# Moving two output products and four base products inside the last head group of an attention kernel

## The chip, the cores and the metric

One core of a Trainium2 chip runs the program. The metric is the device time of one execution in microseconds (us). Five engines work side by side, each through its own instruction queue in order: PE (TensorE: matmuls, and weight loads that run ahead of them), ACT (ScalarE), DVE (VectorE), POOL (GpSimd) and SP, which here only issues DMAs. They wait for one another with semaphores.

## The reference

```
xn = layernorm(A_x)                                   # 2048 x 512
q  = (xn @ wq) as 32 heads of 128
p  = softmax(q k^T / sqrt(128)) ; o = p v             # per head, 2048 keys
s  = concat(o) @ wo                                   # 2048 x 4096 @ 4096 x 512
gate = xn @ W_gate ; up = xn @ W_up
g  = silu((relu(gate) * up) @ W_down)
out = A_x + s * g
```

## The kernel before

The work runs in 128 *blocks*, one for each pair of a head and a quarter of the queries (512 of them). A block has 8 *positions*. At a position PE computes a pair of score tiles (`emit_S_tile`, L1626: two 512-column matmuls) for the position three ahead, ACT turns such a pair into `PT` with one exponential (L1638), and PE multiplies the `PT` of its own position with V (`emit_PV_tile`, L1735: eight matmuls). At the end of a block DVE divides by the row sums (`emit_norm_block`: reciprocal L1655, multiply L1658), and SP transposes the result into `OT_store` by DMA (L1663). The first PV matmul of the next block waits for that multiply, because it overwrites the same accumulator.

All other matrix work is put between these positions as *items* by a plan that is written out by hand: `at(block, position, item)` and `put_p0` fill `plan`, and `side` holds work for DVE, POOL and SP. The loop goes through the blocks position by position and emits, in this order: the score pair, the items of the position, the side work, the PV matmuls. Every engine executes its own instructions in the order of emission.

The accumulators of score pairs and items are three slots of PSUM, taken in turn (`ring_acquire`). Whoever takes a slot waits on PE until the work that last read it is done: the exponential for a score pair, the additions on DVE for an item. When the item at position 0 of a block is marked early (all `emit_x`, `emit_xd` and one-bank items are), the next score pair is emitted right behind it.

Sixteen blocks are four heads, a *head group*. While one group's attention runs, the output product of the group before it is computed by a seven-product scheme of 2 x 2 blocks. The last group, blocks 112 to 127, carries that of group 6; "r3" below is block 112 + 3. Plain products (`emit_one`, L1458, products 1, 7 and 4) take two matmuls of 512 columns for each bank, and DVE adds each bank to two sums at once (`acc`, L1389). Products with a second level (`emit_x`, L1523) take five matmuls, and their remainder (`emit_xd`, L1554 and L1555) two more. The sums are the four tiles `s_acc[:, J, i]`, J from 0 to 3.

Sums that are complete become *base* products: `emit_base(J, i)` multiplies one quarter of a sum by g on DVE (`scalar_tensor_tensor`, L1587), and POOL adds x to it (L1592). g and x had been moved out to DRAM and come back transposed, as `gT` and `xT`. The function `reload_g` issues these DMAs on SP: its first half stands at r3 position 5, its second half at r5 position 1. Each half is four transposing DMAs, gT and xT in turn (L1146, L1147). The wait of a base product reads

```
_wait_all(dve, [os_tok[(J, i)], sem_gr.cur()])
```

where `sem_gr.cur()` stands for every gT reload that was issued before this point of the program, not for the columns that the product reads. The products (0, 0) to (0, 3) read the column groups 0 and 1 of gT, which are those of the first half.

SP's queue in these blocks holds, in order: the K load for the head that starts at r8 (L366; it is emitted at r3 position 5 and waits for the last score pair of the head before, which PE computes at r3 position 4), the first half of the reload, a V load (L371), the transposes of r3 and r4 (L1663), the second half, a load of gN (L1149), and the transposes of r5 and r6.

Of the kernel before, what the change touches and what calls it, by code (L numbers as in the profile page):

```python
# [52 lines left out]
def bass_recurrent_scan__mha_block_cached__glu_gated_reglu__prompt_kernel(  # L53
# [63 lines left out]
    with ExitStack() as es:  # L117
# [1361 lines left out]
        left = {}  # L1479
# [381 lines left out]
        def at(b, p, *items):  # L1861
            plan.setdefault((b, p), []).append(list(items))
# [5 lines left out]
        side = {}  # L1868
# [4 lines left out]
        def put_p0(b, it):  # L1873
            assert b not in osteps
            osteps[b] = it
            if it[0] is emit_x or it[0] is emit_xd or it[1] == 1:
                early.add(b)

        xsteps = (0, 2, 3)
        for g in range(NG - 1):  # L1880
            b0 = (g + 1) * GB
            half = g < NG - 2
            if half and g:
                order = ((2, 0), (1, 2), (7, 4), (6, 6), (5, 10), (3, 14))
                left[g] = len(order) + 4
                for k, r in ((0, 8), (2, 12), (3, 13)):
                    put_p0(b0 + r, (emit_one, 1, g, 4, k // 2, k % 2))
                at(b0 + 3, 6, (emit_one, 1, g, 4, 0, 1))
                early.add(b0 + 9)
                for j, r in order:  # L1890
                    x_at.add(b0 + r)
                    put_p0(b0 + r, (emit_x, 0, g, j, 0))
                    for k in (1, 2):
                        at(b0 + r, 5 if k == 2 and r in (2, 4) else xsteps[k], (emit_x, 0, g, j, k))
                    put_p0(b0 + r + 1, (emit_xd, 2, g, j))
                    side.setdefault((b0 + r - 2, 6 if r in (4, 6) else 4), []).append((prep_x, g, j, 0))
                    side.setdefault((b0 + r - 1, 1), []).append((prep_x, g, j, 1))
                for (r, p), c, i in (((-5, 4), 0, 0), ((-5, 4), 1, 0), ((2, 0), 0, 1), ((2, 2), 0, 2), ((3, 1), 1, 1),
                                     ((3, 3), 1, 2), ((8, 1), 0, 3), ((10, 5), 1, 3)):
                    side.setdefault((b0 + r, p), []).append((emit_ox, g, c, i))  # L1900
                moves = [((1, 2), store_sum, 0), ((4, 1), store_sum, 4), ((5, 2), load_sum, 2), ((6, 1), store_sum, 5),
                         ((6, 6), load_sum, 0)]
                if g == 1:
                    moves.append(((0, 1), store_sum, 2))
                else:
                    moves += [((0, 5), load_sum, 4), ((2, 1), load_sum, 5)]
                if g < NG - 3:
                    moves.append(((16, 1), store_sum, 2))
                for (r, p), fn, a in moves:
                    side.setdefault((b0 + r, p), []).append((fn, a))  # L1910
                continue
            split = {} if g == 0 else {3: 6} if half else {3: 5, 8: 4}
            if g == 0:
                full, part, xs = {0: (1, 0), 12: (1, 1), 2: (7, 0), 6: (7, 1)}, (1, 3, 7, 13), {2: 4, 6: 8, 5: 10, 3: 14}
            elif half:
                full, part, xs = {0: (1, 0), 2: (1, 1), 3: (7, 0), 8: (7, 1)}, (1, 9, 12, 13), {2: 4, 6: 6, 5: 10, 3: 14}
            else:
                full, part, xs = {0: (1, 0), 2: (1, 1), 3: (7, 0), 6: (7, 1)}, (1, 7), {2: 4, 6: 8, 5: 10, 3: 12}
                at(b0 + 9, 4, (emit_one, 2, g, 4, 1, 0))
            for r, (j, q) in full.items():  # L1920
                if r in split:
                    put_p0(b0 + r, (emit_one, 1, g, j, q, 0))
                    at(b0 + r, split[r], (emit_one, 1, g, j, q, 1))
                else:
                    put_p0(b0 + r, (emit_one, 2, g, j, q, 0))
            for k, r in enumerate(part):
                put_p0(b0 + r, (emit_one, 1, g, 4, k // 2, k % 2))
            left[g] = len(full) + len(split) + len(part) + 4 + (not half)
            for j, r in xs.items():
                x_at.add(b0 + r)  # L1930
                put_p0(b0 + r, (emit_x, 0, g, j, 0))
                for k in (1, 2):
                    at(b0 + r, xsteps[k], (emit_x, 0, g, j, k))
                put_p0(b0 + r + 1, (emit_xd, 2, g, j))
            px = ((2, 1), (4, 4), (7, 1), (11, 1))
            if g == 0:
                px = ((2, 1), (5, 3), (8, 5), (11, 3))
            elif not half:
                px = (px[0], ((5, 4))) + ((8, 5), (10, 5))
            for k, (j, (r, p)) in enumerate(zip((2, 6, 5, 3), px)):  # L1940
                side.setdefault((b0 + r, p), []).append((prep_x, g, j, 0))
                r, p = max((r, p), (xs[(2, 6, 5)[k - 1]] + 1, 1)) if k else (r, p)
                side.setdefault((b0 + r, p), []).append((prep_x, g, j, 1))
            ox = ((0, 0), (0, 3), (1, 0), (1, 2), (1, 3), (1, 4), (9, 6), (9, 4))
            if not half:
                ox = ((0, 2), (4, 4), (4, 5), (0, 5), (5, 2), (5, 3), (9, 2), (9, 3))
            elif g:
                ox = ((0, 2), (0, 3), (0, 4), (3, 2), (3, 3), (3, 4), (8, 5), (8, 1))
            for k, (r, p) in enumerate(ox):
                side.setdefault((b0 + r, p), []).append((emit_ox, g, *((k // 3, k % 3) if k < 6 else (k - 6, 3))))  # L1950
# [20 lines left out]
        for b in range(NBLK):  # L1971
            pr, r = (b - 2) // 8 + 1, (b - 2) % 8
# [49 lines left out]
        fb = GB * (NG - 1)  # L2022
# [3 lines left out]
                           (4, 6, 5, 2)):  # L2026
            side.setdefault((fb + r, p), []).append((add_kept, a, i))
        for i in range(4):
            side.setdefault((fb + 7, 2 + i), []).append((emit_base, 0, i))
        for i, part, (r, p) in ((1, 0, (11, 1)), (1, 1, (11, 2)), (3, 0, (11, 2)), (3, 1, (11, 3)), (0, 0, (11, 2)), (0, 1, (11, 4)), (2, 0, (11, 4)), (2, 1, (11, 5))):  # L2030
            side.setdefault((fb + r, p), []).append((emit_finish, i, part))
        for k, (J, i) in enumerate(((3, 1), (3, 3), (1, 1), (1, 3))):
# [28 lines left out]
        for gp in range(LAG, TOTP):  # L2061
# [7 lines left out]
            split = not ahead and not items and bq < GB  # L2069
# [107 lines left out]
```

## Time and profile before

| | |
|---|---|
| time, median of 3 runs | 1234.03 us (1233.92 to 1234.49) |
| the profiled execution's own time | 1233.89 us |
| its span, first to last instruction | 1232.6 us (1.29 us lie around it) |
| PE busy | 1227.8 us (100%) |
| ACT busy | 1041.9 us (85%) |
| DVE busy | 873.5 us (71%) |
| POOL busy | 834.5 us (68%) |
| granted TensorE clock | 0.999 |

The blocks are found in the trace by the reciprocal of L1655, which ends each of them: r3 ends at 1121.71 us of the span, r5 at 1137.45, r6 at 1145.39, r7 at 1153.06. Times below are us from the start of the span. Where a row merges several instructions, its time is the stretch they cover together. [...]

### The profile page before, as it was taken

The numbers are of one execution on the slowest core, as the hardware profiler recorded it, in microseconds if no ns is written. First come the engines' busy times: TensorE is split into PE (matmuls) and PEld (weight loads), VectorE is DVE, ScalarE is ACT, GpSimd is POOL, SyncE is SP. The second block draws the span as 40 slices with busy tenths as digits, with TensorE's granted clock in tenths as the row PEclk, the third lists the DMA queues.
The fourth block names the chain that finished last, engine by engine and source line by source line (L and its number), as shares of the span: only waits on it lengthen the run. The fifth ranks groups of instructions, "written<-read, shape, count | busy, mean of one in ns | idle before, by whom it ended". The sixth has DMA issues, their size and how long they took to land.

```text
span 1232.6 us, 29291 instructions
## 1 busy us (share of the span) xinstructions
PE 1227.8 (100%) x11927; PEld 817.3 (66%) x11927; DVE 873.5 (71%) x1324; ACT 1041.9 (85%) x1110; POOL 834.5 (68%) x946
## 2 busy tenths in 40 slices
PE   9999999999999999999999999999999999999998
PEld 5466666776666666666666666666666666666665
DVE  7668787667676776677666776677676767675587
ACT  4457877668899999999999999999999999989994
POOL 3355876313668767787688776986788767668368
PEclk9999999999999999999999999999999999999999
DMA  9812331323232555246522753255532562348616
GB/s 276 159 31 37 75 79 28 52 48 91 57 53 52 142 120 131 49 90 173 173 41 50 212 153 94 51 142 163 155 52 52 184 190 48 53 103 167 122 35 142
DMA packets 285061, 127.21 MB, mean 103 GB/s; under 512 B 253696, under 2 KB 279552, under 8 KB 280064
## 3 DMA queue, kind: packets, MB, share of 16 engines
q1 hardware_dynamic: 283584, 124.55, 43.6%
q8 instruction: 95, 1.56, 0.6%
q10 hardware_dynamic: 1344, 0.79, 0.2%
q14 instruction: 38, 0.31, 0.1%
HBM read 57.93 MB, written 25.17 MB: 67 GB/s over the span
## 4 chain that ended last, share of the span: by engine, by line
PE 99%; DVE 0%; DMA 0%; issue 0%
PE ps_acc L1735 38%; PE ps_r L1626 36%; PE ps_r L1060 5%; PE ps_r L1178 3%; PE ps_r L1523 3%; PE ps_r L1239 3%; PE ps_r L924 2%; PE ps_r L739 2%; PE ps_r L743 2%; PE ps_r L1458 2%; PE ps_acc L842 1%; PE ps_r L1767 1%; PE ps_r L1554 1%; PE ps_r L1555 1%; PE ps_r L1848 0%; PE ps_r L551 0%
## 5 line engine op out<-in xcount | busy, mean ns | idle before, releaser
L1638 ACT ACTIVATE PT<-ps_r 128x1024 bf16<-128x1024 f32 x1024 | 990.1, 1025 | 124.9 <-PE ps_r L1626 111.1
L1735 PEld LDWEIGHTS ps_acc<-V_sb,PT 128*128 128x128 bf16 x8192 | 544.8, 98 | 225.5 <-issue 28.1
L1735 PE MATMUL ps_acc<-V_sb,PT 128*128 128x129 bf16 x8192 | 630.0, 220 | 0.0
L1626 PE MATMUL ps_r<-QT_sb,KT_sb 128*128 128x512 bf16 x2048 | 617.6, 379 | 0.0
L1065 DVE TENSOR_TENSOR UVR<-UVR,ps_r 128x512 f32<-128x512 f32 (+1 forms) x228 | 168.8, 756 | 96.8 <-PE ps_r L1060 91.9
L1626 PEld LDWEIGHTS ps_r<-QT_sb,KT_sb 128*128 128x128 bf16 x2048 | 158.9, 98 | 35.4 <-ACT PT L1638 31.6
L1389 DVE TENSOR_TENSOR s_acc<-s_acc,ps_r 128x1024 f32<-128x1024 f32 x108 | 131.2, 1218 | 17.1 <-PE ps_r L1458 9.1
L1405 DVE TENSOR_TENSOR s_acc<-s_acc,ps_r 128x512 f32<-128x512 f32 x152 | 101.0, 683 | 28.3 <-PE ps_r L1523 23.9
L1658 DVE TENSOR_TENSOR Onorm<-ps_acc,rz_sb 128x512 bf16<-128x512 f32 x127 | 87.8, 691 | 4.4
L1489 POOL TENSOR_TENSOR TI<-OX 128x512 f16<-128x512 f16 x38 | 43.1, 1155 | 70.6 <-issue 69.2
L1655 DVE RECIPROCAL rz_sb<-ps_acc 128x4 f32<-128x4 f32 x127 | 23.1, 182 | 85.7 <-PE ps_acc L1735 84.0
L1025 POOL TENSOR_TENSOR TI<-xn_sb 128x512 f16<-128x512 f16 x48 | 55.8, 1163 | 40.7 <-PE ps_r L1060 40.7
L1065 DVE TENSOR_TENSOR QT_sb<-UVR,ps_r 128x512 bf16<-128x512 f32 x72 | 49.5, 687 | 43.0 <-PE ps_r L1060 40.6
L1489 POOL TENSOR_TENSOR TI<-OT_store 128x512 f16<-128x512 bf16 (+1 forms) x38 | 45.6, 1221 | 31.9 <-PE ps_r L1523 16.1
L1333 POOL TENSOR_TENSOR WX<-Wo_sb 128x512 f16<-128x512 bf16 x7 | 8.1, 1154 | 81.3 <-DVE Wo_sb L1323 42.4
L1025 POOL TENSOR_TENSOR TI<-xn_sb,TI 128x512 f16<-128x512 f16 x48 | 55.9, 1165 | 0.0
L1025 POOL TENSOR_TENSOR TI<-xnT 128x512 f16<-128x512 bf16 x36 | 41.6, 1155 | 14.0 <-PE ps_r L1060 14.0
L1060 PE MATMUL ps_r<-TI,SI 128*128 128x512 f16 x126 | 47.8, 379 | 0.0
L1523 PE MATMUL ps_r<-TI,SI 128*128 128x512 f16 x114 | 43.2, 379 | 0.0
L1025 POOL TENSOR_TENSOR TI<-xnT,TI 128x512 f16<-128x512 bf16 x36 | 41.6, 1155 | 0.0
L1154 POOL TENSOR_SCALAR gB<-gB 128x512 bf16<-128x512 bf16 x14 | 20.8, 1484 | 30.4 <-DVE gB L1184 30.4
L1133 POOL TENSOR_TENSOR UVR<-UVR,UVR 128x512 f32<-128x512 f32 x24 | 29.8, 1273 | 11.8 <-DVE UVR L1065 11.8
(236 smaller groups left out, 1434.6 us busy)
## 6 DMA issues: line engine op xcount, KB each, us to landing
sums<-s_acc SPq DMA_DIRECT2D x20, 1024.0 KB, 4.5
s_acc<-sums SPq DMA_DIRECT2D x18, 1024.0 KB, 5.8
V_sb<-in_A_v_cache_dram SPq DMA_DIRECT2D x32, 512.0 KB, 4.3
Wq_sb<-in_A_wq_dram SPq DMA_DIRECT2D x16, 256.0 KB, 4.5
Wo_sb<-in_A_wo_dram SPq DMA_DIRECT2D x8, 512.0 KB, 3.9
out_dram<-g_sb SPq DMA_DIRECT2D x4, 512.0 KB, 4.5
KR<-sums SPq DMA_DIRECT2D x4, 512.0 KB, 4.5
OT_store<-Onorm SPq DMA_TRANSPOSE x127, 3.0
```

The source lines that it names most:

```text
L1025: return sem_ui.sig(pool.tensor_tensor(dst, x, y, o))
L1060: return sem_up.sig(pe.matmul(dst, lhs, rhs, start=start, stop=stop, skip_group_check=True))
L1065: dve.tensor_tensor(dst, x, ps, ALU.add))
L1178: ins = pe.matmul(ps_r[:, bank, :], L(i), R(i), start=(i == 0), stop=(i == HC - 1))
L1389: t = sem_opa.sig(dve.tensor_tensor(dst, dst, sb, op))
L1405: t = dve.tensor_tensor(dst, dst, sb, op)
L1489: return sem_oi.sig(pool.tensor_tensor(dst, x, y, o))
L1523: return sem_op.sig(pe.matmul(dst, lhs, rhs, start=start, stop=stop, skip_group_check=True))
L1626: ins = pe.matmul(ps_r[:, 2 * s + tt, :], KT_sb[h % 2][:, t * 128:(t + 1) * 128], QT_sb[qt_slot[(h, Q)]][:], start=True, stop=True)
L1638: act.activation(PT[pb][:], ps_r[:, 2 * s:2 * s + 2, :], ACTF.Exp, scale=scale / WSC)
L1658: dve.tensor_tensor(Onorm[ob][:], o_ap, rz_sb[:].to_broadcast([128, 4, Dh]), ALU.mult))
L1735: ins = pe.matmul(o_ap, PT[pb][:, tt, j * 128:(j + 1) * 128], V_sb[vb][:, t, 0:VW], start=(t == 0 and j % 2 == 0), stop=(t == KT - 1 and j ...
```

## The change

Three things move, all in the last head group, and nothing is added or left out.

- Product 7 of the first query half stood with one bank at r3 position 0 and one at r3 position 5; both banks now stand at r3 position 0.
- Product 7 of the second half had both banks at r6 position 0; now one is at r6 position 0 and one at r6 position 6. Product 4 of the second half had both banks at r9 position 4; now one is at r7 position 6 and one at r9 position 6.
- The base products (0, 0) to (0, 3) stood at r7, positions 2 to 5. Now (0, 0) and (0, 1) stand at r6, positions 3 and 4, and (0, 2) and (0, 3) at r7, positions 2 and 3.

```diff
                 full, part, xs = {0: (1, 0), 2: (1, 1), 3: (7, 0), 6: (7, 1)}, (1, 7), {2: 4, 6: 8, 5: 10, 3: 12}
-                at(b0 + 9, 4, (emit_one, 2, g, 4, 1, 0))
+                split = {6: 6}
+                for r, e in ((7, 0), (9, 1)):
+                    at(b0 + r, 6, (emit_one, 1, g, 4, 1, e))
...
-            left[g] = len(full) + len(split) + len(part) + 4 + (not half)
+            left[g] = len(full) + len(split) + len(part) + 4 + 2 * (not half)
...
         for i in range(4):
-            side.setdefault((fb + 7, 2 + i), []).append((emit_base, 0, i))
+            side.setdefault((fb + 6 + i // 2, (3, 4, 2, 3)[i]), []).append((emit_base, 0, i))
```

`split` names the products whose second bank stands apart, with its position; it was `{3: 5, 8: 4}` for this group. `left[g]` only counts the products of a group, and nothing waits for the count of this one.

## The prediction

> **What bounds the kernel now.** I read the busy shares first, then the chain of waits, then the busy time of each engine block by block.
>
> ```profile
> PE 1227.8 (100%) x11927; PEld 817.3 (66%) x11927; DVE 873.5 (71%) x1324; ACT 1041.9 (85%) x1110; POOL 834.5 (68%) x946
> ...
> PE 99%; DVE 0%; DMA 0%; issue 0%
> ```
> ```profile
> 1113.76:1121.71 7.95, 7.95 (x85) 5.51 (x84) 3.27 (x5) 7.52 (x9) 6.30 (x6) 1.00 0.66 180
> ...
> 1137.45:1145.39 7.94, 7.94 (x85) 5.57 (x84) 3.18 (x5) 7.40 (x9) 2.33 (x5) 1.00 1.05 219
> 1145.39:1153.06 7.67, 7.67 (x83) 5.30 (x82) 5.46 (x7) 7.47 (x9) 4.04 (x4) 1.00 1.14 211
> ...
> 1161.35:1169.79 8.44, 8.44 (x87) 5.70 (x86) 5.84 (x7) 7.57 (x9) 2.71 (x5) 1.00 0.08 17
> ```
>
> PE never rests, and the chain is PE to 99%, so whatever makes PE wait lengthens the kernel one for one. The second fence is the table by stretch for the four blocks that the change touches, r3, r6, r7 and r9 (columns: length, then busy time of PE, weight loads, DVE, ACT, POOL, then clock, DMA share, GB/s). In r6 DVE is busy for only 3.18 of 7.94 us, which looks like room for two more instructions. That is throughput; the question is what these instructions wait for.
>
> The timelines of r6 and r7 follow, of PE, of DVE, and of SP from r3 on.
>
> ```profile
> 1137.68 1.03 PE L1458 MATMUL ps_r<-OX,WX 128*128 128x512 f16 x4
> 1138.54 0.62 PE L1735 MATMUL ps_acc<-V_sb,PT 128*128 128x129 bf16 x8
> ...
> 1145.62 0.59 PE L1458 MATMUL ps_r<-OT_store,WX 128*128 128x512 bf16 x2
> 1146.20 0.60 PE L1626 MATMUL ps_r<-QT_sb,KT_sb 128*128 128x512 bf16 x2
> ```
> ```profile
> 1146.20 0.11 PEld L1626 LDWEIGHTS ps_r<-QT_sb,KT_sb 128*128 128x128 bf16 x2 [0.48 <-ACT PT L1638]
> ...
> 1146.64 1.07 PE L1735 MATMUL ps_acc<-V_sb,PT 128*128 128x129 bf16 x16
> ```
> ```profile
> 1138.31 2.35 DVE L1389 TENSOR_TENSOR s_acc<-s_acc,ps_r 128x1024 f32<-128x1024 f32 x2
> 1145.39 0.18 DVE L1655 RECIPROCAL rz_sb<-ps_acc 128x4 f32<-128x4 f32 x1 [4.73 <-PE ps_acc L1735]
> 1145.61 0.69 DVE L1658 TENSOR_TENSOR Onorm<-ps_acc,rz_sb 128x512 bf16<-128x512 f32 x1
> 1146.25 1.22 DVE L1389 TENSOR_TENSOR s_acc<-s_acc,ps_r 128x1024 f32<-128x1024 f32 x1
> 1147.43 3.46 DVE L1587 SCALAR_TENSOR_TENSOR s_acc<-s_acc,gT 128x512 f32<-128x512 f32 x4
> ```
> ```profile
> 1118.16 2.99 SPq L366 DMA_TRANSPOSE KT_sb<-in_A_k_cache_dram  x1
> 1121.25 3.25 SPq L1146 DMA_TRANSPOSE gT<-out_dram  x1
> 1124.54 2.08 SPq L1147 DMA_TRANSPOSE xT<-in_A_x_dram  x1
> 1126.66 2.35 SPq L1146 DMA_TRANSPOSE gT<-out_dram  x1
> 1129.06 1.78 SPq L1147 DMA_TRANSPOSE xT<-in_A_x_dram  x1
> 1130.90 0.57 SPq L371 DMA_DIRECT2D V_sb<-in_A_v_cache_dram  x1
> 1131.52 4.98 SPq L1663 DMA_TRANSPOSE OT_store<-Onorm  x2
> 1136.61 2.19 SPq L1146 DMA_TRANSPOSE gT<-out_dram  x1
> 1139.14 2.22 SPq L1147 DMA_TRANSPOSE xT<-in_A_x_dram  x1
> 1141.42 2.21 SPq L1146 DMA_TRANSPOSE gT<-out_dram  x1
> 1143.67 3.10 SPq L1147 DMA_TRANSPOSE xT<-in_A_x_dram  x1
> ```
> ```profile
> gT<-out_dram SPq DMA_TRANSPOSE x1, 5.9
> xT<-in_A_x_dram SPq DMA_TRANSPOSE x1, 5.3
> ```
> ```profile
> 1149.02 5.11 POOL L1592 TENSOR_TENSOR s_acc<-s_acc,xT 128x512 f32<-128x512 f32 x4 [9.16 <-DMA xT<-in_A_x_dram]
> ```
>
> The reader is to see three things. First, SP issues without a pause from 1118.16 on; each transposing DMA holds it for about 2.2 us, and the fourth gT reload is issued only at 1141.42. The two rows on landing are those of the last gT and the last xT: they land 5.9 and 5.3 us after issue, at 1147.32 and 1148.97. POOL's row confirms the second: it waits 9.16 us for xT and starts at 1149.02, 0.05 us after the landing. Second, in the kernel before the base products start at 1147.43, 0.11 us after the last gT has landed, so their wait is paid nowhere. Third, DVE reaches the end of its additions in r6 at 1138.31 + 2.35 = 1140.66 and then sits idle, with nothing queued but the reciprocal of the block's end.
>
> **The change part by part.**
>
> *The matmuls.* Items in these four blocks take (2+2), 4, 2 and 4 plain matmuls before, and 4, (2+2), (2+2) and 2 after: 14 each time. Four cost 0.86 us (1137.68 to 1138.54), two 0.43. Sum: 0. DVE's additions move along, one of 1.22 us for each bank: also 0.
>
> *The balance with ACT.* Without items PE needs less for a position than ACT does for its exponential, so after a long plain stretch PE waits a little for a slot. At r7 the weight load shows 0.48 us of such a wait, but PE itself loses 1146.20 - (1145.62 + 0.43) = 0.15 us.
>
> ```profile
> PEld ps_r L1626 <- ACT PT L1638: 2.7, 7, 0.5
> ```
>
> That row of the waits (stretch from r3 to r10) has all seven of them, 2.7 us as the weight loads see it. Items at position 6 take this from r7 and r8. But r3 loses its item at position 5, and r6 becomes an early block; I expect about 0.15 us each at the start of r4 and of r6. If every wait is scaled as at r7 (0.15 for 0.48), all seven hold 0.8 us: bounds -0.8 and +0.3. Value: 0 up to r7, and behind it -0.2, because ACT will have caught up during the stall below.
>
> *SP's queue.* Both banks of product 7 at r3 position 0 put 0.43 us more ahead of the last score pair of the head, for which the K load waits.
>
> ```profile
> SPq L366 <- PE ps_r L1626: 3.4, 1, 3.4
> ```
>
> SP waited 3.4 us for exactly that before 1118.16 and is without a gap afterwards, so every DMA behind it goes 0.43 us later: the last gT lands at 1147.75. Bounds: 0, if the backlog swallows it, and 0.43. I take 0.43.
>
> *The base products at r6.* Here the change adds a wait. Both halves of the reload are emitted before r6, so `sem_gr.cur()` at r6 position 3 means all four gT loads. DVE comes to that instruction at about 1140 and waits until 1147.75. Queued behind it on DVE, in order: the second base product, the addition of the new item of r6 position 6, reciprocal and multiply of r6, the addition of r7's first item. PE waits for two of these: the item at r7 position 0 takes the slot that the position 6 item used (slots go in turn: item, pair of position 7, pair of r7 position 0, item), and the first PV of r7 waits for the multiply. Step by step, with 0.05 us from landing to start as on POOL:
>
> - first base product starts 1147.80; the four rows of L1587 below start between 1147.4 and 1149.2, 0.6 us apart, so the addition starts 1.2 later, at 1149.00, and takes 1.22: 1150.22;
> - reciprocal and multiply: 0.22 (1145.39 to 1145.61) plus 0.69: 1151.13;
> - from the end of a multiply to the PV matmul that waits for it: 0.19 us, as at r4 (1121.92 + 0.69 to 1122.80);
> - by the slot, PE resumes at 1150.22 + 0.19 = 1150.41, then 0.43 for the item and 0.43 for the score pair: 1151.27; by the multiply, PV starts at 1151.32.
>
> ```profile
> L1587 DVE SCALAR_TENSOR_TENSOR s_acc<-s_acc,gT x4: 682/688/1644, 1147.4 to 1149.2; 128x512 f32<-128x512 f32 x4
> ```
> ```profile
> 1121.92 0.69 DVE L1658 TENSOR_TENSOR Onorm<-ps_acc,rz_sb 128x512 bf16<-128x512 f32 x1
> ...
> 1122.80 1.07 PE L1735 MATMUL ps_acc<-V_sb,PT 128*128 128x129 bf16 x16
> ```
>
> The PV of r7 that started at 1146.64 starts at 1151.32: +4.7 us. Losses ahead of r7 are swallowed by it, since its end is set by SP. Less the 0.2 us: **+4.5**. Bounds: the four gT loads took 4.8 to 5.9 us to land, so a quick one takes off 1.1, and an unmoved K load 0.43: +3.0. A slow issue (3.25 for 2.2, as the first gT) adds 1.0: +5.5.
>
> ```profile
> DMA to landing us min/median/max: 4.8/5.2/5.9
> ```
>
> POOL's own wait for xT (until about 1149.4) is in front of nothing that PE needs before r8; it was there before. The base products left in r7 run behind the stall in DVE's idle time. SP waits for r6's multiply some 4 us longer with a K load behind it, for a head whose start is delayed as much.
>
> Sum: 1233.89 + 4.5 = 1238.4 for the profiled execution; the median of the runs lies 0.14 above it, which I leave inside the rounding.
>
> **The rivals.**
>
> *A. PE comes back slow.* PE will stand still from about 1146.1 to 1150.4, over 4 us; nothing like it is in this trace after the start. At the start PE comes from rest:
>
> ```profile
> 0.76 4.00 PE L485 MATMUL ps_r<-const-bfloat16-1.0 128*128 128x256 bf16 x18 [0.76 <-PEq L2162]
> ```
>
> 18 matmuls of 256 columns take 4.00 us, 0.22 each, where by the 0.86 us for four of 512 columns 0.11 would be due: 2.0 us lost, although the clock column says 1.00 there. If a rest of this length is enough to bring that back, 1238.4 + 2.0 = 1240.4. Against it: the rest before the start is longer than any in the kernel, so the trace doesn't say where the limit lies. [...]
>
> *B. The wait is hidden: not slower.* If the base products find gT landed, or PE needs nothing from DVE in time, only the balance is left: -0.8 to +0.3, so 1233.1 to 1234.2, and 1233.8 as the likeliest. The point from which this decides: the last gT must land about 4.7 us sooner, by 1142.6, which is 1.2 us after its issue. The shortest landing is 4.8. For it speaks only that I might read the order of emission wrongly, or that the trace's landing times are late; POOL's start speaks against that.
>
> *C. Faster by more.* The seven waits for ACT, 2.7 us even as the weight loads see them, would have to vanish whole: 1231.2.
>
> **How the numbers follow.** From no change this kernel's measurement can tell about 0.2%, 2.5 us. The forecast has 0.60 (its own range 1236.9 to 1239.4), A 0.20, B 0.16, C 0.04. Slower by over 0.2% takes in the forecast and A: 0.80; within: B, 0.16; faster: 0.04. The range 1236.6 to 1240.9 holds the forecast and A and leaves out B and C.
>
> **What would show it.** In the changed profile: DVE's first L1587 in r6 with an idle of some 7 us put down to the gT DMA; r6's reciprocal not at the end of its PV matmuls but some 4.5 us later; PE idle between r7's first score pair and its item; L1587 two and two; r4 and r6 starting with a wait for ACT of some 0.4 us on the weight load; SP's K load 0.4 us later. Rows of 0.2 us and more for PV pairs behind the stall would speak for A. A span within 1 us of 1232.6 would make the prediction wrong, and so would a DVE wait at r6 that ends before 1145.

## The result and the profile after

The changed kernel takes 1240.86 us (median of 6 executions, 1239.54 to 1241.95) where the kernel before takes 1234.03 (6 executions, 1233.89 to 1234.56): a ratio of 1.0055, 95% interval 1.0045 to 1.0065. It is slower by 6.8 us: 2.5 us above the predicted time, and inside the stated range by 0.04 us. The executions of the changed kernel differ by 2.4 us from one another, those of the kernel before by 0.7. The profiled execution took 1241.95 us, with a span of 1240.6, 8.0 more than before.

The chain of waits of the changed kernel, which was PE to 99%, now has DMA issue and a DMA in it:

```profile
PE 97%; SPq 2%; DMA 1%; DVE 0%; issue 0%; DVEq 0%
```

The longest pieces of that chain between 1142 and 1152.8 us, in order of time (start, length, what; all us):

```profile
1142.06 6.29 DMA gT<-out_dram
1149.05 0.69 DVE s_acc L1587
1149.74 1.14 DVE s_acc L1389
1150.92 1.03 PE ps_r L1458 x2
1151.96 0.85 PE ps_r L1626 x2
```

That is the predicted path: the last gT load, a base product, the addition of the item of r6 position 6, and PE at the first item of r7. The timelines of DVE, PE and SP behind it:

```profile
1137.84 0.18 DVE L1655 RECIPROCAL rz_sb<-ps_acc 128x4 f32<-128x4 f32 x1 [4.14 <-PE ps_acc L1735]
...
1138.70 1.22 DVE L1389 TENSOR_TENSOR s_acc<-s_acc,ps_r 128x1024 f32<-128x1024 f32 x1
1148.44 1.29 DVE L1587 SCALAR_TENSOR_TENSOR s_acc<-s_acc,gT 128x512 f32<-128x512 f32 x2 [8.52 <-DMA gT<-out_dram]
1149.65 1.21 DVE L1389 TENSOR_TENSOR s_acc<-s_acc,ps_r 128x1024 f32<-128x1024 f32 x1
1150.78 0.18 DVE L1655 RECIPROCAL rz_sb<-ps_acc 128x4 f32<-128x4 f32 x1
1150.99 0.69 DVE L1658 TENSOR_TENSOR Onorm<-ps_acc,rz_sb 128x512 bf16<-128x512 f32 x1
```
```profile
1145.71 0.59 PE L1626 MATMUL ps_r<-QT_sb,KT_sb 128*128 128x512 bf16 x2
...
1150.92 1.03 PE L1458 MATMUL ps_r<-OT_store,WX 128*128 128x512 bf16 x2 [4.62 <-DVE s_acc L1389]
```
```profile
1118.83 2.51 SPq L366 DMA_TRANSPOSE KT_sb<-in_A_k_cache_dram  x1
1121.44 3.14 SPq L1146 DMA_TRANSPOSE gT<-out_dram  x1
...
1142.06 2.69 SPq L1146 DMA_TRANSPOSE gT<-out_dram  x1
```

DVE is idle for 8.52 us ahead of its first base product, and the row names the gT load. PE stands still between the score pair of r7 position 0 and its item for 4.62 us.

Then comes what the forecast had given to rival A. The two matmuls of the item take 1.03 us together where they took 0.59, and the table by stretch shows the clock (columns: length, busy time of PE, weight loads, DVE, ACT, POOL, then PEclk, DMA share, GB/s):

```profile
1146.80:1150.20 3.40, 0.00 (x0) 0.00 (x0) 1.76 (x3) 0.59 (x1) 0.20 (x1) 0.99 0.98 147
1150.20:1153.60 3.40, 2.68 (x14) 1.58 (x15) 3.06 (x5) 0.75 (x1) 2.07 (x2) 0.50 0.80 215
1153.60:1156.92 3.32, 3.32 (x22) 2.22 (x21) 0.82 (x2) 1.29 (x2) 2.58 (x2) 0.50 0.01 1
1156.92:1160.00 3.08, 3.08 (x33) 2.15 (x32) 0.00 (x0) 2.88 (x4) 0.00 (x0) 1.00 0.24 54
```

From about 1150.1 to 1156.9 the granted clock is 0.50, which is called half rate below. PE has work from 1150.92, so 6.0 us of work at half rate, and 3.0 us lost if that work would take half as long at 1.00. The clock column, which said 1.00 at the start of the kernel where matmuls were just as slow (0.22 us for 256 columns there, 0.83 for two of 512 here, from 1150.92 to 1151.75), does show this one.

Where the 8.0 us of the span went, from the starts of the same instructions in both traces:

| | us |
|---|---|
| drift between the executions ahead of r3 (the reciprocal at its start: 1113.76 and 1114.00) | 0.24 |
| waits for ACT at the starts of r4 and r6 (last score pair before the rest: 1145.19 and 1145.71, less the drift) | 0.28 |
| the rest at r7 (its first item: 1145.62 and 1150.92, less the 0.52 above) | 4.78 |
| r7 behind the rest: half rate, and the item it got from r9 (0.43) | 3.19 |
| r8 to the end: the item that r9 gave away (-0.43), and less waiting for ACT | -0.49 |
| sum | 8.00 |

### The profile page after: what moved, and what is told of

It reads as the page before. It is cut to its first block, busy times and chain, and to the rows that moved or that the text cites. A ratio compares the mean times of both kernels' runs of the same rounds, so it can differ in the third digit from the quotient of the medians.

```text
span 1240.6 us, 29293 instructions
## 1 busy us (share of the span) xinstructions
PE 1231.2 (99%) x11927; PEld 819.4 (66%) x11927; DVE 873.0 (70%) x1324; ACT 1042.3 (84%) x1110; POOL 835.3 (67%) x946
## 4 chain that ended last, share of the span: by engine, by line
PE 97%; SPq 2%; DMA 1%; DVE 0%; issue 0%; DVEq 0%
PE ps_acc L1735 37%; PE ps_r L1626 35%; PE ps_r L1060 5%; PE ps_r L1178 3%; PE ps_r L1523 3%; PE ps_r L1239 3%; PE ps_r L924 2%; PE ps_r L739 2%; PE ps_r L743 2%; PE ps_r L1458 2%; PE ps_acc L842 1%; PE ps_r L1767 1%; PE ps_r L1555 1%; PE ps_r L1554 1%; SPq L1146 1%; DMA gT<-out_dram 1%
```

## The experiments

The theory: all of the loss comes from `sem_gr.cur()`. The base products at r6 wait for gT columns that they don't read, DVE's queue stands behind them, PE rests, and its granted clock is 0.50 from 1150.1, 0.8 us before the end of the rest, to 1156.9. The rivals: the output products cost something where they stand now; or two more DVE instructions in r6 do.

**The changed kernel again.**

> The changed kernel as it is, timed again. [...] So: 1238.5 to 1242, a spread of over 2 us where the kernel before spreads over 0.7, and longer times where the mean clock is lower. Rival (the slow return is a fixed part of the program): all runs within 0.7 us of 1241.

Measured: 1239.26, 1240.21, 1240.65, 1235.65 and 1240.12 us; ratio 1.0040 (1.0027 to 1.0053). The spread of 5 us is larger than expected, 1235.65 lies below the expected range, and the longer times don't always have the lower granted clock (1239.26 at 0.998, 1240.21 at 0.999). What sets the length of half rate from one execution to the next is not shown by any run. In the profiled one (1239.26) the last gT is issued at 1141.13 and lands 5.8 us later, and PE's rest ends at 1149.53. The low one, 1235.65, has no profile; that its reload landed early is a guess. Of the half rate this profile shows more than the first:

```profile
1147.43:1150.85 3.42, 1.32 (x12) 0.75 (x13) 3.39 (x6) 0.24 (x1) 2.09 (x2) 1.00 0.96 244
1150.85:1154.27 3.42, 3.20 (x23) 2.40 (x22) 1.77 (x3) 1.80 (x2) 2.28 (x3) 0.50 0.25 47
1154.27:1158.00 3.73, 3.73 (x41) 2.70 (x41) 0.40 (x1) 3.49 (x4) 0.47 (x1) 1.00 0.42 88
```

PE came back at a granted clock of 1.00 at 1149.53, and the clock fell to 0.50 1.3 us later, in the middle of PE's work, for 3.42 us. So half rate lasted 3.42 us here and 6.8 in the first profile. In the 3.42 us just before this fall PE was busy for 1.32, 39%.

**The base products back.**

```diff
-            side.setdefault((fb + 6 + i // 2, (3, 4, 2, 3)[i]), []).append((emit_base, 0, i))
+            side.setdefault((fb + 7, 2 + i), []).append((emit_base, 0, i))
```

> The changed kernel with the four base products back at r7, positions 2 to 5; the output products stay where the change put them. Theory (all of the loss comes from the base products' wait for the reload): 1233.7 to 1234.4, no rest of PE, no clock under 1.00 in r6 to r8, DVE's first base product at about 1148, waiting under 1 us for gT. Rival (moving the output products costs something of its own): 1236 or more.

Measured: 1233.96 us (10 executions, 1233.75 to 1234.54), ratio 0.9999 (0.9990 to 1.0008). The output products cost nothing in their new places. DVE's base products start at 1147.86, right behind the addition before them, with no wait for gT:

```profile
1146.72 1.22 DVE L1389 TENSOR_TENSOR s_acc<-s_acc,ps_r 128x1024 f32<-128x1024 f32 x1
1147.86 3.45 DVE L1587 SCALAR_TENSOR_TENSOR s_acc<-s_acc,gT 128x512 f32<-128x512 f32 x4
```

The balance with ACT, which the moves could have helped, is unchanged. The weight loads of r3 to r9 wait for ACT as often as before (2.7 us, 7 times):

```profile
PEld ps_r L1626 <- ACT PT L1638: 2.6, 7, 0.5
```

**The base products alone.** The kernel before with

```diff
-            side.setdefault((fb + 7, 2 + i), []).append((emit_base, 0, i))
+            side.setdefault((fb + 6 + i // 2, (3, 4, 2, 3)[i]), []).append((emit_base, 0, i))
```

> The kernel before with only the base products moved as in the change. Theory: DVE waits for gT until about 1147.4 as the K load isn't delayed; no item of r6 position 6 stands between, so PE reaches the second score pair of r7 and waits only at the first PV for r6's multiply, 2.3 us after the first base product: 1149.7 for 1146.64, a rest of PE of about 3.0 us and +3.0 us: 1237. [...] Rival (the item split carries the loss, the base products are free): 1234.0.

Measured: 1240.20, 1239.41, 1237.51, 1239.22 and 1240.22 us, ratio 1.0040 (1.0027 to 1.0053). The base products carry the loss by themselves. As expected PE stops one step later, at the first PV, and for the multiply:

```profile
1150.32 1.89 PE L1735 MATMUL ps_acc<-V_sb,PT 128*128 128x129 bf16 x16 [3.34 <-DVE Onorm L1658]
```

But only one of the five is near 1237, and its granted clock is 1.000. A sixth execution took 4682.30 us at a granted clock of 1.000; it has no profile, what held it is not known, and it is left out of the ratio. In the profiled execution the last gT landed 6.3 us after an issue at 1141.67, the rest of PE was 3.34 us, and the granted clock was 0.50 for 6.83 us, from 1149.12, 1.20 us before the end of the rest, to 1155.95:

```profile
1145.70:1149.12 3.42, 1.28 (x6) 0.21 (x3) 1.06 (x2) 2.46 (x3) 0.00 (x0) 1.00 1.23 168
1149.12:1152.54 3.42, 2.00 (x17) 1.97 (x19) 3.39 (x6) 0.00 (x0) 2.26 (x2) 0.50 0.97 223
1152.54:1155.95 3.41, 3.41 (x21) 2.29 (x21) 0.53 (x1) 2.05 (x2) 2.58 (x2) 0.50 0.00 0
```

The expected 1237 was the rest alone. Half rate came on top of it, and in the 3.42 us before the fall PE had still been busy for 1.28 (37%).

**Only the wait taken away.** The two halves of the reload count on semaphores of their own, and nothing else differs from the changed kernel:

```diff
-                sem_gr.sig(sp.dma_start_transpose(gT[:, c, :], out2[:, cs]))
+                sem_gr[half].sig(sp.dma_start_transpose(gT[:, c, :], out2[:, cs]))
...
-            _wait_all(dve, [os_tok[(J, i)], sem_gr.cur()])
+            _wait_all(dve, [os_tok[(J, i)], sem_gr[c // 2].cur()])
```

(`sem_xr`, for POOL, in the same way, so that POOL's wait for xT is taken away together with DVE's for gT.)

> The changed kernel, but the two halves of the reload count on semaphores of their own, and a base product waits only for the half that holds its columns. Everything stands where the change put it. Theory (the loss is the wait for columns that aren't read): no wait of DVE for gT in r6, base products at about 1140 to 1143, no rest of PE, 1233.5 to 1234.2, so no difference from the kernel before that can be told. Rival (two more DVE instructions in r6, or the places of the items, cost by themselves): 1235 or more.

Measured: 1234.03 us (11 executions, 1233.86 to 1234.46), ratio 0.9999 (0.9990 to 1.0008). The base products run at r6 without a wait, and r6's reciprocal follows its PV matmuls:

```profile
1138.42 1.22 DVE L1389 TENSOR_TENSOR s_acc<-s_acc,ps_r 128x1024 f32<-128x1024 f32 x1
1139.56 1.33 DVE L1587 SCALAR_TENSOR_TENSOR s_acc<-s_acc,gT 128x512 f32<-128x512 f32 x2
1144.29 1.22 DVE L1389 TENSOR_TENSOR s_acc<-s_acc,ps_r 128x1024 f32<-128x1024 f32 x1 [3.41 <-PE ps_r L1458]
1145.63 0.18 DVE L1655 RECIPROCAL rz_sb<-ps_acc 128x4 f32<-128x4 f32 x1
```

So the whole loss is the wait, and with the wait gone the change is worth nothing that can be measured. This run takes away two waits; that DVE's for gT is the one that counts is read from the changed kernel's profile, where the chain runs through gT and DVE and the only wait of PE from r3 to r10 is the one for DVE's addition (4.62 us).

**Rests of three lengths.** The last kernel, with additions into a dead buffer ahead of the base products, which hold DVE with no DMA:

```diff
+        def hold_dve(sizes):
+            w = WX[1][:].rearrange("p k h d -> p (k h d)").bitcast(BF16)
+            z = s_acc[:, 0].rearrange("p i q -> p (i q)")
...
+            for n in sizes:
+                _wait(dve, t)
+                t = sem_opa.sig(dve.tensor_tensor(w[:, 0:n], z[:, 0:n], z[:, 0:n], ALU.add))
...
+        side.setdefault((fb + 6, 3), []).append((hold_dve, (2048, 2048, 640)))
```

The rest alone would give 1234.0 us plus its length. Half rate for 3.42 us, as in the second profile of the changed kernel, would add an estimated 1.7 to it, half of its length, and that of the first profile 3.0. So estimated rests of 1.6, 2.6 and 3.8 us give 1235.6, 1236.6 and 1237.8 without half rate; with it the second kernel would take 1238.3 for 3.42 us of it, the third 1239.5 to 1240.8. The profiles up to here have half rate with rests of 3.34 and 4.62 us.

> The kernel in which base products wait only for their own half of the reload, with three additions of 2048, 2048 and 640 elements into a dead buffer put on DVE at r6 position 3, ahead of the base products. They hold DVE as the reload did, without any DMA, and let PE rest for an estimated 1.6 us at the start of r7 (5.3 us of additions, of which 3.7 fall into DVE's idle time). [...] Rival (any rest of PE brings the slow return): 1237 and more.

> As the run before, with additions of 2048, 2048 and 1536 elements: an estimated rest of 2.6 us. [...]

> As the run before, with additions of 2048, 2048, 2048 and 448 elements: an estimated rest of 3.8 us. [...] Rival (it takes a DMA in the chain): 1237.8 in all.

Measured, against 1234.13 us (16 executions) of the kernel before; the rest is PE's idle time in the profile, at the first item of r7:

| rest, us | executions | median (lowest to highest), us | above before, less the rest | ratio |
|---|---|---|---|---|
| 1.57 | 10 | 1235.86 (1235.71 to 1236.67) | 0.2 | 1.0015 (1.0005 to 1.0024) |
| 2.50 | 7 | 1238.24 (1236.81 to 1239.40) | 1.6 | 1.0031 (1.0020 to 1.0042) |
| 3.74 | 4 | 1240.25 (1239.77 to 1240.82) | 2.4 | 1.0049 (1.0034 to 1.0064) |

With a rest of 1.6 us eight of ten executions lie within 0.3 us of the rest alone (1235.7); the other two are 0.7 and 1.0 us above it at a granted clock of 1.000, for a reason that is not known. With 2.5 us two of seven lie at 1236.8 and 1236.9 and four at 1238.1 to 1238.5: by these times the rest alone (1236.6), or about the estimated 1.7 us of half rate more. The seventh, 1239.4, is 2.8 above the rest alone. With 3.7 us all four, at 1239.8 to 1240.8 where the rest alone gives 1237.9, have half rate by their times. One execution of each kernel has a profile. For the others the mean granted clock agrees (1.000 in the two low ones with 2.5 us, 0.998 or 0.999 in the other five), but 0.999 also occurs without a fall, as in the profile before. The stretches in the three profiles, of which the second and the third have a fall:

```profile
1144.44:1147.86 3.42, 1.85 (x22) 1.13 (x20) 3.35 (x6) 2.77 (x3) 1.65 (x2) 1.00 1.25 147
...
1149.71:1153.10 3.39, 3.39 (x42) 2.44 (x39) 1.24 (x3) 3.05 (x5) 2.59 (x2) 1.00 0.91 225
```
```profile
1144.90:1148.32 3.42, 1.28 (x12) 0.65 (x10) 3.38 (x4) 2.20 (x3) 1.28 (x1) 1.00 1.11 173
1148.32:1151.74 3.42, 3.06 (x17) 1.95 (x18) 3.08 (x6) 1.02 (x1) 1.32 (x3) 0.50 1.14 239
1151.74:1155.00 3.26, 3.26 (x38) 2.33 (x36) 0.44 (x1) 2.44 (x3) 2.57 (x2) 1.00 0.14 23
```
```profile
1145.38:1148.80 3.42, 0.90 (x11) 0.41 (x8) 3.35 (x5) 1.94 (x2) 0.42 (x1) 1.00 1.15 170
1148.80:1152.22 3.42, 2.20 (x9) 1.10 (x10) 3.08 (x5) 0.28 (x1) 2.16 (x2) 0.50 0.93 217
1152.22:1155.62 3.40, 3.40 (x26) 2.57 (x24) 1.30 (x3) 1.77 (x2) 2.56 (x2) 0.50 0.16 31
```

In the kernel with the rest of 1.57 us, the 3.42 us that end with the rest still have 1.85 us of work (54%), as little as any 3.42 us can have with this rest, and the clock stays at 1.00. In the others the 3.42 us before the fall have 1.28 (37%) and 0.90 us (26%), and the clock falls to 0.50. In these kernels DVE is held by its own additions and not by a DMA, and they differ from one another only in the length of the additions, which leaves the rest itself as the cause: in the profiles the fall came with 2.50 and 3.74 us of it, and not with 1.57.

## Why the prediction was right, and where it was wrong

*The wait at the base products: right.* DVE waits at r6 position 3 for the last gT load, the first item of r7 waits for the slot, and the multiply comes late; taking the wait away alone gives back all of it. The forecast for this part was +4.7 us at the first PV of r7. Measured at the first item, PE is idle for 4.62 us in one profile (the item comes 4.78 us later than it would) and for 3.34 in another. The forecast let the multiply decide by 0.05 us over the slot; in the first profile the slot decides, because the item and the score pair behind it run at half rate.

*SP's queue: the K load was later as predicted, the queue behind it was not.* The K load was issued 0.43 us later as predicted (1118.16 to 1118.83, less 0.24 of drift). But it then held SP for 2.51 us where it had held it for 2.99, and the first gT load was issued at 1121.44 where it had been 1121.25, which is less than the drift. So the delay was gone there, and the lower bound of 0 was the right value for it. What moved the last gT load is scatter further down the queue: less the drift, it was issued 0.40 us later than before in the first profile (1142.06 against 1141.42) and 0.41 us sooner in the second profile of the same kernel (1141.13, drift 0.12). It landed 6.3 and 5.8 us after its issue, where the trace before has 4.8 to 5.9.

*The balance with ACT: right at r4 and r6.* They do start with waits of 0.48 and 0.45 us on the weight load, of which 0.28 us reach PE together where 0.3 was expected. Behind the rest the forecast had -0.2; the table above leaves -0.06 for it (-0.49 without the moved item's -0.43).

*The likeliest case: wrong.* The forecast of 1238.4 was the rest alone. Rival A, the slow return, is what happens in both profiles of the changed kernel and, by their times, in most other executions. Two steps failed. First its chance of 0.20: the prediction said that the trace doesn't show how long a rest has to be, and then took over 4 us to be more likely too short than long enough. Three profiles fell with rests of 2.50, 3.34 and 3.34 us and with PE busy for 37 to 39% of the 3.42 us before the fall, and with 2.5 us of rest five of seven executions have half rate by their times. Second its price: 2.0 us, from the start of the kernel, where 4.0 us are slow. Here half rate lasted 3.42 us in two profiles and about 6.8 in three, and cost an estimated 3.0 us in the profiled execution: 1238.4 becomes 1241.4 with that, against 1241.95 measured for this execution and a median of 1240.86. The range holds the result only because A was taken into it, and narrowly: its upper end is 1240.9, and three of the six executions lie above that. That A's own 1240.4 is the nearest figure is in part luck, as its 2.0 us, taken from another place, happen to lie between the 1.6 us that the median has on top of a rest of 2.5 and the 3.0 of the first profile.

*Rival B, not slower, and rival C fell:* the output products by themselves change nothing (1233.96).

## What to carry to other kernels

An instruction moved earlier into an idle engine is free only if everything that it waits for is there by then: look up in the trace when the last thing that its semaphore counts lands, and who is queued behind it. A wait on "all loads so far" should be cut to the load that is read; here a semaphore for each half took 6 to 7 us away. And a stall of PE can cost more than its length: here rests of 2.50 and 3.74 us cost 1.6 and 2.4 us on top of it (medians of seven and of four executions), one of 1.57 us 0.2, with no half rate in its profile.

## What the runs showed of the hardware

In five profiles the granted clock of PE fell from 1.00 to 0.50 at r7. Before each fall, over 3.42 us, which is the shorter of the two lengths that half rate had, PE was busy for 0% (the changed kernel), 26% (rest of 3.74 us), 37% (rest of 2.50 us), 37% (the base products alone) and 39% (the changed kernel again); in the last of them PE had been at work again for 1.3 us when the clock fell. In the kernel with the rest of 1.57 us PE was busy for 54% of the 3.42 us that end with the rest, and the clock stayed at 1.00. Shares between 39 and 54% were not run, and what decides on a fall is not shown.

The clock returned to 1.00 after 3.42 us in two profiles and after about 6.8 in three. Where it returned after 3.42 us, PE was busy for 3.06 or 3.20 of them; where it took 6.8, PE was busy for 2.00, 2.20 or 2.68 of the first 3.4 us.

The K load, a transposing DMA, held SP's queue for 2.99 us in the kernel before and for 2.51 in the changed kernel, where it was issued 0.43 us later, so that the next issue didn't move. It was 2.49 to 2.56 us in four profiles of kernels with the later issue (the changed kernel twice, the base products back, only the wait taken away), and 2.92 and 2.99 in the two without; the reason is not shown.
